# The first batch's preparation written out in engine order, its two head groups staggered, its conversions and table transfers moved

## The chip, the cores and the metric

The kernel runs on one core of one Trainium2 chip. The metric is the device time of one execution in microseconds. The engines of the core are TensorE (PE in the profile, PEld for its weight loads), VectorE (DVE), ScalarE (ACT), GpSimd (POOL) and SyncE (SP, which only issues transfers here).

## The reference

Batch 8, 8 heads, 576 tokens, 64 columns a head, 32 packed queries, model width 512, hidden width 2048, all float32.

```python
p_packed = sm_attn(p, k, v)               # 32 packed queries attend to 576 keys
out = sm_attn(q, p_packed, p_packed)      # 576 queries attend to the 32 packed values
x = out.transpose(0, 2, 1, 3).reshape(B, S, H * D)
X = np.fft.fft(np.fft.fft(x, axis=1), axis=2)
u = x + np.real(X).astype(np.float32)
un = (u - mean(u)) / np.sqrt(var(u) + 1e-06)
return u + np.maximum(un @ w_ch1, 0.0) @ w_ch2
```

## The kernel before

**Accuracy by splitting.** Large products use float32 operands split into a rounded high part (ScalarE, `split`, L97) and the remainder (VectorE or GpSimd, L98): `three` (L230) makes three products of the parts. Names in h and l are such pairs (uh and ul, fh and fl, gh and gl, wr_h and wr_l).

**Front and feed-forward.** `front(b)` (L235) prepares batch b. It works on two groups of four heads, g = 0 and 1, in steps named by letters in ORDER (L40), the first string for batch 0, the second for all others: transfers K, I, V, Q, B, L, W; S scores and exponents; X turned scores; p packed values (with the block diagonals bd, bdh, bdl on GpSimd and ScalarE); d their transposition and split; U the queries' products, turned back into blocks of 32 by VectorE; g the values' spectrum (basis product, multiplication with the tables turn, split into gh and gl); e subtracts the maximum and takes exponents; m subtracts the mean; a scales and transposes; f folds the rows about the middle (even and odd sums); r the folds' last few columns; h splits the folds into fh and fl, and xl, ol. Then follow the wave products (py), their spectrum (pz) and the values (px), the sums pe and qe (L554 to L558), the rows of u with their sum (L561), and statistics (L205: negative mean, squares on ScalarE, a power on GpSimd). EN, EF, ES choose VectorE (0) or GpSimd (1) for some steps: in batch 0 group 1's subtractions, scaling and folds are on GpSimd, and both groups' r.

The generator gives a `yield` where the caller may go on with other work. The main part is `ffn` (L650) for tiles of 512 rows: for each of 16 blocks j of the hidden width an up product (L669), ReLU and split (hh, hl, L673 and L674), and a down product (L684). Every `step` in it advances the next batch's front by one `yield`. Up products write one PSUM bank (tag ph), so one must have been read by hh and hl before the next begins.

**Weights** come as packed words: `fetch` transfers a block to a staging place, `halves_of` makes two ScalarE operations of it (L167, L168), `joined` one VectorE operation (L172). `wsplits` (L640) then splits each block into wr_h on ScalarE and wr_l on GpSimd, for each tile anew. Six blocks are converted before `ffn` begins, the others within the first tile.

**Order of work.** Within `tc.manual_schedule` TensorE, VectorE, ScalarE and GpSimd follow the written order. Outside it, as batch 0's front, the first rows' centring, transposition and split (L744 to L749) and the first conversions are, the framework's scheduler orders each engine's queue by itself, and may draw later written work ahead. `after(n, what)` does a thing n steps later inside `ffn`, and at once before that.

[...]

Of the kernel before, what the change touches and what calls it, by code (L numbers as in the profile page):

```python
# [9 lines left out]
F32 = mybir.dt.float32  # L10
# [7 lines left out]
P = 128  # L18
S = 576
# [12 lines left out]
EF = (((0, 0, 0, 0), (1, 1, 0, 0)), ((0, 0, 0, 0), (0, 0, 0, 0)), ((0, 0, 0, 0), (0, 0, 0, 0)))  # L32
# [7 lines left out]
ORDER = ("K0 K1 I0 V0 V1 Q0 Q1 B0 L0 W0 W1 W2 W3 S X p0 p1 d0 d1 U W4 W5 W6 W7 W8 g0 g1 e0 e1 m0 m1 a0 a1 f0 r0 h0 f1 r1 h1",  # L40
         "S y X y p0 p1 y d0 d1 y g0 y U y g1 y e0 y e1 y y m0 y a0 y m1 y a1 y f0 y r0 y h0 y f1 y r1 y h1 y y")
# [34 lines left out]
def tile_kernel(ctx, tc, kpT, qT, v, w1, w2, tabs, tabR, tabB, tabT, sel, ident_d, out):  # L76
# [45 lines left out]
    def load_base():  # L122
        nc.gpsimd.dma_start(basis, tabB)
        nc.sync.dma_start(turn, tabT)
# [80 lines left out]
    def statistics(key):  # L205
        st, u = stat_of[key], u_of[key]
        nc.vector.tensor_scalar(st[:, 1:2], st[:, 0:1], -1.0 / DM, None, ALU.mult)  # L207

        def squares():
            junk = work.tile([P, DM], F32, tag="tmp", name="junk", bufs=3)  # L210
            nc.scalar.activation(junk, u, AF.Square, bias=st[:, 1:2], scale=1.0, accum_out=st[:, 2:3])  # L211
# [23 lines left out]
    def front(b):  # L235
# [3 lines left out]
        eos, fs, sums = {}, {}, {}  # L239
# [71 lines left out]
        def packed(g):  # L311

            if g not in vts:
                load_values(g)
            vt = vts[g]
            po = bank("po")
            for c in range(5):
                kk = P if c < 4 else D
                for h in range(4):
                    nc.tensor.matmul(  # L320
                        po[h * NPK:(h + 1) * NPK, :D], e1T[g][:kk, c, h * NPK:(h + 1) * NPK],
                        vt[:kk, c, h * D:(h + 1) * D], start=(c == 0), stop=(c == 4),
                        tile_position=(0, h * NPK))
            pp2 = work.tile([P, 2, D], F32, tag="pp2", name="pp2")
            nc.vector.tensor_scalar(pp2, po[:, :D].unsqueeze(1).to_broadcast([P, 2, D]), rinv[g], None, ALU.mult)
            pp2s[g] = pp2
            bd = work.tile([P, 4, D], F32, tag="tmp", name="bd", bufs=3)
            nc.gpsimd.tensor_tensor(bd, pp2[:, 0:1, :].to_broadcast([P, 4, D]),
                                    bmask.unsqueeze(2).to_broadcast([P, 4, D]), ALU.mult)

            def diagonals():
                bdh[g] = work.tile([P, 4 * D], F32R, tag="bdh", name="bdh")
                bdl[g] = work.tile([P, 4 * D], F32R, tag="bdl", name="bdl")
                split(bdh[g], bdl[g], bd.rearrange("p a d -> p (a d)"), nc.gpsimd)

            after(1, diagonals)

        def packed_parts(g):
# [5 lines left out]
            nc.vector.tensor_copy(t, tp[:, :P])  # L344
            ppT[g] = t
# [9 lines left out]
        def queries(*gs):  # L355
# [10 lines left out]
            for c, w in ((1, slice(16, 18)), (0, slice(0, 16))):  # L366
                for g in reversed(gs):
                    nc.vector.transpose(s2s[g][:, w, :].rearrange("p a k -> p (a k)"), s2T[g][c])
# [25 lines left out]
        def values_spectrum(g):  # L394

            hi = work.tile([P, 2, N2], F32R, tag="gh", name="gh")
            lo = work.tile([P, 2, N2], F32R, tag="gl", name="gl")

            TW = (nc.gpsimd, nc.vector)
            prod = []  # L400
            for t in range(2):
                pg = bank("pg")
                nc.tensor.matmul(pg[:, :N2], pph[g], basis[:, t, :], start=True, stop=False)

                nc.tensor.matmul(pg[:, :N2], ppl[g], basis[:, t, :], start=False, stop=True)
# [8 lines left out]
            gh[g], gl[g] = hi, lo  # L414
            after(1, lambda: split(hi, lo, prod[0], TW[TL[min(b, 2)]]))

        def weights(g):

            engs[g].tensor_tensor(s2s[g], s2s[g], broadcast(zs[g]), ALU.mult)
            a = work.tile([P, S], F32, tag="att", name="a", bufs=ATT)  # L420
            nc.vector.transpose(a, s2s[g].rearrange("p a k -> p (a k)"))
            as_[g] = a

        def folded(g):
# [3 lines left out]
            f = work.tile([P, FW], F32, tag="att", name="f", bufs=ATT)  # L428
# [8 lines left out]
            eos[g], fs[g] = eo, f  # L437

        def folded_rest(g):
# [17 lines left out]
            sm.tensor_copy(fe3[:, :, 15:16], ec[:, 143:144].unsqueeze(1).to_broadcast([P, 3, 1]))  # L457
            sm.tensor_copy(fo3[:, :, 30:31], oc[:, 143:144].unsqueeze(1).to_broadcast([P, 3, 1]))
            sm.memset(f[:, FR + 99:FR + 101], 1.0 / 32)
            sm.memset(fo3[:, :, 31:33], 0.0)  # L460
            sm.tensor_scalar(f[:, FA:FA + 33], a[:, 256:289], 2.0, 1.0 / 16, ALU.mult, ALU.add)
            sm.tensor_scalar(f[:, FA + 33:FA + 64], a[:, NE + 256:S], 2.0, 1.0 / 16, ALU.mult, ALU.add)
# [5 lines left out]
        def folded_parts(g):  # L468
# [4 lines left out]
            nc.scalar.copy(fh[g], f)  # L473
            xl[g] = work.tile([P, 256], F32R, tag="xl", name="xl")
# [3 lines left out]
            fl[g] = work.tile([P, FW], F32R, tag="fl", name="fl")  # L478
            nc.vector.tensor_tensor(fl[g], f, fh[g].bitcast(F32), ALU.subtract)

        parts = {"S": lambda _: scores(0, 1), "U": lambda _: queries(0, 1), "X": lambda _: turned_scores(0, 1),
                 "s": scores, "t": turned_scores, "p": packed, "d": packed_parts, "q": queries, "e": less_one, "m": less_mean, "g": values_spectrum, "a": weights, "f": folded, "r": folded_rest,
                 "h": folded_parts,
                 "L": lambda _: load_tables(), "B": lambda _: load_base(), "K": load_keys, "V": load_values,
                 "Q": load_queries, "I": lambda _: nc.sync.dma_start(ident, ident_d),
                 "W": lambda i: fetch(i // 2, i % 2), "D": load_weights}
# [6 lines left out]

        yh, yl, yr = [], [], []
        for t, base in enumerate((0, FO)):
            nr = NRC[t]
            hi = work.tile([P, 2, N2], F32R, tag="att", name="yh", bufs=ATT)
            lo = work.tile([P, 2, N2], F32R, tag="att", name="yl", bufs=ATT)
            for c in range(2):
                py = bank("py")  # L500
                for g in range(2):
                    w = slice(base + c * P, base + (c + 1) * P)
                    three(py[:, :N2], fh[g][:, w], fl[g][:, w], gh[g][:, t, :], gl[g][:, t, :], g == 0, g == 1)
                split(hi[:, c, :], lo[:, c, :], py[:, :N2])
            py = bank("pyr")
            for g in range(2):
                w = slice(base + 256, base + 256 + nr)
                three(py[:nr, :N2], fh[g][:, w], fl[g][:, w], gh[g][:, t, :], gl[g][:, t, :], g == 0, g == 1)
            h = work.tile([P, DM], F32R, tag="tmp", name="yr_h", bufs=3)
            nc.scalar.copy(h[:nr, :N2], py[:nr, :N2])  # L510
            st = work.tile([P, N2], F32R, tag=f"yr{t}", name="yr", bufs=1)
            nc.vector.scalar_tensor_tensor(st[:nr], h[:nr, :N2].bitcast(F32), selB[:nr], py[:nr, :N2],
                                           ALU.mult, ALU.add)
            yh.append(hi)
            yl.append(lo)
            yr.append(st)
            yield

# [30 lines left out]
        for c in range(2):  # L549
            A, Bs = spectrum(0, c), spectrum(1, c)  # L550
            yield
            px = value(xh, xl, slice(1 - c, 256, 2))
            pe = work.tile([P, DM], F32, tag="tmp", name="pe", bufs=3)
            nc.vector.tensor_tensor(halves(pe), halves(px), window(A, allp), ALU.add)  # L554
            px = value(oh, ol, slice(1 - c, 256, 2))
# [3 lines left out]
            for key, sign in (((b, "E", c), 1.0), ((b, "O", c), -1.0)):  # L559
                new_u(key)  # L560
                nc.vector.scalar_tensor_tensor(u_of[key], qe, sign, pe, ALU.mult, ALU.add,  # L561
                                               accum_out=stat_of[key][:, 0:1])
            statistics((b, "E", c))
            statistics((b, "O", c))
            yield (None, "rest")[c]
# [175 lines left out]
    for at in gen0:  # L741
        if at == "rest":
            break
    cur = Turned(tiles[0][1])  # L744
    for i in range(4):
        cur.less(i)
        for move in cur.moves(i):
            move()
        cur.parts(i)  # L749
    spare.clear()  # L750
    rest = gen0
    for j in range(ORDER[0].count("D"), LEAD):
        load_weights(j)
    ready, splits = [], wsplits()
    next(splits)
    next(splits)
# [139 lines left out]
```

## Time and profile before

| | us |
|---|---|
| median of 3 runs | 997.16 |
| their range | 995.86 to 998.61 |
| the profiled execution | 998.08 |
| its span, first to last instruction | 996.3 |

The mean granted clock of TensorE in the profiled execution was 0.983. In rows of a timeline stand the start, the duration, engine, line, operation, out<-in with shapes, a count, and in brackets the idle time before and what ended it. In rows of a table of stretches stand the stretch, its length, then busy time and count of PE, PEld, DVE, ACT and POOL, the granted clock, the share of the DMA engines and GB/s. Of the page's 40 slices each stands for 24.9 us; a digit is a tenth.

### The profile page before, as it was taken

How to read it: one execution, taken by the hardware profiler on the slowest of the kernel's cores; microseconds unless marked ns; L12 is line 12 of the kernel's file. 1: busy time of each engine (PE TensorE's matmuls, PEld its weight loads, DVE VectorE, ACT ScalarE, POOL GpSimd, SP SyncE). 2: the span in 40 equal slices, each digit the busy share in tenths (PEclk: the TensorE clock that was granted, in tenths of full speed). 3: DMA queues.
4: the chain of work that ended last, by engine and by line, in shares of the span. 5: the costliest groups of instructions: out<-in, count | busy, mean ns of one | idle time of the engine just before them, and what ended most of it. 6: DMA issues, size and time to landing. Idle time of an engine off the chain costs nothing.

```text
span 996.3 us, 15070 instructions
## 1 busy us (share of the span) xinstructions
PE 953.2 (96%) x5588; PEld 784.4 (79%) x5588; DVE 552.2 (55%) x1227; ACT 469.9 (47%) x942; POOL 477.1 (48%) x420
## 2 busy tenths in 40 slices
PE   5189999999999999999999999999999999999998
PEld 2077778778887888788887888788878888888886
DVE  4866885559354845577546846594648562123112
ACT  4447786444453445445544445435434453343332
POOL 3705643455346534554445434653555354544443
PEclk9589999999999999999999999999999999999999
DMA  9206552410042002200240024101410010011001
GB/s 357 116 6 231 157 175 65 160 36 1 8 135 74 1 1 89 101 1 16 65 157 1 3 59 134 43 1 50 139 49 1 22 64 1 1 31 54 1 1 43
DMA packets 28170, 65.94 MB, mean 66 GB/s; under 512 B 5494, under 2 KB 12992, under 8 KB 28096
## 3 DMA queue, kind: packets, MB, share of 16 engines
q1 hardware_dynamic: 27120, 63.53, 19.2%
q0 software_dynamic: 976, 1.44, 0.5%
q8 instruction: 44, 0.72, 0.3%
q14 instruction: 30, 0.25, 0.1%
HBM read 48.70 MB, written 9.44 MB: 58 GB/s over the span
## 4 chain that ended last, share of the span: by engine, by line
PE 91%; DVE 4%; ACT 2%; POOL 1%; DMA 1%; issue 1%; DVEq 0%; POOLq 0%; ACTq 0%
PE ph L669 38%; PE acc L684 38%; PE po L320 1%; PE s L263 1%; PE px L233 1%; PE px L232 1%; PE px L231 1%; PE py L231 1%; PE e1tp L297 1%; PE py L232 1%; PE py L233 1%; PE pz L231 1%; PE pz L233 1%; PE pz L232 1%; PE s2T L263 1%
## 5 line engine op out<-in xcount | busy, mean ns | idle before, releaser
L98 POOL TENSOR_TENSOR wr_l<-w1f,wr_h 128x512 fp32r<-128x512 f32 x144 | 199.5, 1386 | 280.7 <-ACT wr_h L97 228.6
L674 DVE SCALAR_TENSOR_TENSOR hl<-ph,hh 128x512 fp32r<-128x512 f32 x144 | 99.1, 688 | 341.3 <-ACT hh L673 340.9
L98 POOL TENSOR_TENSOR wr_l<-w2f,wr_h 128x512 fp32r<-128x512 f32 x144 | 190.3, 1322 | 160.1 <-ACT wr_h L97 153.2
L669 PE MATMUL ph<-uh,wr_h 128*128 128x512 f32 (+1 forms) x580 | 228.6, 395 | 4.3 <-DVE hl L674 2.7
L684 PE MATMUL acc<-wr_h,hh 128*128 128x512 f32 x576 | 226.1, 393 | 0.0
L684 PE MATMUL acc<-wr_l,hh 128*128 128x512 f32 x576 | 225.4, 391 | 0.0
L669 PE MATMUL ph<-uh,wr_l 128*128 128x512 f32 (+1 forms) x580 | 225.4, 389 | 0.0
L684 PE MATMUL acc<-wr_h,hl 128*128 128x512 f32 x576 | 225.2, 391 | 0.0
L669 PE MATMUL ph<-ul,wr_h 128*128 128x512 f32 (+1 forms) x580 | 220.8, 389 | 1.1 <-DVE stat L207 1.1
L673 ACT ACTIVATE hh<-ph 128x512 fp32r<-128x512 f32 x144 | 86.3, 599 | 209.2 <-PE ph L669 195.1
L669 PEld LDWEIGHTS ph<-uh,wr_h 128*128 128x128 f32 x580 | 108.9, 188 | 39.0 <-ACT gh L97 6.1
L669 PEld LDWEIGHTS ph<-uh,wr_l 128*128 128x128 f32 x580 | 108.8, 188 | 23.4 <-POOL wr_l L98 0.3
L684 PEld LDWEIGHTS acc<-wr_h,hl 128*128 128x128 f32 x576 | 108.1, 188 | 23.1
L669 PEld LDWEIGHTS ph<-ul,wr_h 128*128 128x128 f32 x580 | 109.0, 189 | 22.0 <-DVE stat L207 1.3
L684 PEld LDWEIGHTS acc<-wr_h,hh 128*128 128x128 f32 x576 | 108.1, 188 | 22.0
L684 PEld LDWEIGHTS acc<-wr_l,hh 128*128 128x128 f32 x576 | 108.2, 188 | 21.4
L97 ACT CAST wr_h<-w1f 128x512 fp32r<-128x512 f32 x144 | 89.0, 618 | 55.6 <-POOL wr_l L98 52.8
L97 ACT CAST wr_h<-w2f 128x512 fp32r<-128x512 f32 x144 | 88.4, 614 | 10.0 <-PE acc L684 7.2
L231 PE MATMUL py<-gh,fh 128*128 128x258 f32 x64 | 19.5, 305 | 26.3 <-ACT fh L473 26.3
L211 ACT ACTIVATE junk<-ubuf,stat 128x512 f32<-128x512 f32 x36 | 25.6, 714 | 27.6 <-DVE stat L207 27.6
L98 POOL TENSOR_TENSOR gl<-turned,gh 128x516 fp32r<-128x516 f32 x16 | 24.8, 1551 | 27.3 <-ACT gh L97 27.3
L215 POOL TENSOR_TENSOR stat<-stat,mhalf 128x1 f32<-128x1 f32 x36 | 23.6, 671 | 25.6 <-DVE stat L214 25.6
(198 smaller groups left out, 1257.8 us busy)
## 6 DMA issues: line engine op xcount, KB each, us to landing
kp<-kpT SPq DMA_DIRECT2D x16, 608.0 KB, 3.9
out<-ubuf SPq DMA_DIRECT2D x36, 256.0 KB, 2.1
vt<-v SPq DMA_DIRECT2D x14, 640.0 KB, 5.1
wst<-w SPq DMA_DIRECT2D x17, 512.0 KB, 3.6
qt<-qT SPq DMA_DIRECT2D x14, 576.0 KB, 4.9
raw<-flip SPq DMA_DIRECT2D x208, 32.0 KB, 1.8
ubuf<-w SPq DMA_DIRECT2D x9, 512.0 KB, 3.9
w1f<-w SPq DMA_DIRECT2D x3, 512.0 KB, 13.8
```

Source lines behind the costliest of these rows:

```text
L97: nc.scalar.copy(hi, src)
L98: (lo_eng or nc.vector).tensor_tensor(lo, src, hi.bitcast(F32), ALU.subtract)
L211: nc.scalar.activation(junk, u, AF.Square, bias=st[:, 1:2], scale=1.0, accum_out=st[:, 2:3])
L215: nc.gpsimd.tensor_tensor(st[:, 2:3], st[:, 2:3], mhalf, ALU.pow)
L231: nc.tensor.matmul(o, lh, rh, start=first, stop=False)
L232: nc.tensor.matmul(o, lh, rl, start=False, stop=False)
L233: nc.tensor.matmul(o, ll, rh, start=False, stop=last)
L263: nc.tensor.matmul(res[g][c][at, :w.stop - w.start], lhs(g, h), rhs(g, h, w), start=True, stop=True, tile_position=(r, h * NPK))
L669: nc.tensor.matmul(ph[:, t], l[:, c * P:(c + 1) * P], r[:, c, t], start=(n == 0), stop=(n == 11))
L673: nc.scalar.activation(hh[:, :T], ph[:, :T], AF.Relu)
L674: nc.vector.scalar_tensor_tensor(hl[:, :T], ph[:, :T], 0.0, hh[:, :T].bitcast(F32), ALU.max, ALU.subtract)
L684: nc.tensor.matmul(acc[i], l[:, w], r, start=(j == 0 and k == 0), stop=(j == NJ - 1 and k == 2))
```

## The change

Batch 0's front, the first six conversions but for their transfers, the first two weight splits and the first tile's centring and transposition move into `manual_schedule`, in a written order. That order lets the two groups follow each other step by step (first group's e and m before the second group's e and m are through, waves of group 0 before group 1's fold). Steps are cut finer for that: c (block diagonals), l (split of the packed values), u (second group's blocks), G, T, z (the parts of g), w and b (of a), x (xl and ol), P (wave products of one group, six PSUM banks open at once).

Of single operations: basis comes through SP into a staging place and is copied by ScalarE (N); the tables' six GpSimd transfers (L) stand behind the block diagonals; the halves of weight blocks (H) stand between front steps and the joins at their places in the main part; group 1's folds go to VectorE; r's two copies and two doublings go to ScalarE, its two constants to GpSimd ahead of the folds; f lies in the space of uh; centring is ScalarE's; squares and the power of the first rows wait for the first steps of `ffn`. For other batches fl comes before xl and ol, and both rows are made before their statistics; the rest is as it was.

```diff
-EF = (((0, 0, 0, 0), (1, 1, 0, 0)), ...
+EF = (((0, 0, 0, 0), (0, 0, 0, 0)), ...
-ORDER = ("K0 K1 I0 V0 V1 Q0 Q1 B0 L0 W0 W1 W2 W3 S X p0 p1 d0 d1 U W4 W5 W6 W7 W8 g0 g1 e0 e1 m0 m1 a0 a1 f0 r0 h0 f1 r1 h1",
+ORDER = ("K0 K1 I0 V0 V1 Q0 Q1 B0 W0 W1 W2 W3 S t0 t1 p0 p1 d0 d1 l0 l1 U N c0 W4 W5 c1 L0 W6 W7 W8 H0 H1 e0 u G0 e1 "
+         "H2 T0 z0 G1 m0 w0 b0 H3 H4 f0 r0 m1 w1 T1 h0 z1 P0 H5 b1 f1 r1 x0 h1 x1 P1",
...
-        nc.gpsimd.dma_start(basis, tabB)
+        nc.sync.dma_start(spot(0, 2, [P, 2, N2]), tabB)
...
-        after(1, squares)
-        after(2, deviation)
+        now_at = steps[0] if steps[0] is not None else key[2]
+        due.append((now_at + 1, squares))
+        due.append((now_at + 2, deviation))
...
+            if b == 0 and g == 1:
+                nc.scalar.copy(t, tp[:, :P])
+            else:
+                nc.vector.tensor_copy(t, tp[:, :P])
...
-            f = work.tile([P, FW], F32, tag="att", name="f", bufs=ATT)
+            if b > 0:
+                f = work.tile([P, FW], F32, tag="att", name="f", bufs=ATT)
+            else:
+                if g == 0:
+                    fs[None] = work.tile([P, 4, 512], F32, tag="uh", name="f", bufs=1).rearrange("p c t -> p (c t)")
+                f = fs[None][:, g * 1024:g * 1024 + FW]
+                constants(f, nc.gpsimd)
...
+                for o, x in doubled:
+                    nc.scalar.activation(o, x, AF.Copy, scale=2.0, bias=1.0 / 16)
+                for o, x in middles:
+                    nc.scalar.copy(o, x.unsqueeze(1).to_broadcast([P, 3, 1]))
...
+        WAVES = [(0, 0), (1, 0), (0, None), (1, None), (0, 1), (1, 1)]
...
+        def waves_of(g):
+            for at in WAVES:
+                if g == 0:
+                    pys[at] = bank("py")
+                wave(*at, (g,))
+                if g == 1:
+                    wave_split(*at)
...
+        if b == 0:
+            pq = None
+            for c in range(2):
+                px = [side_value(n, c) for n in range(2)]
+                AB = spectrum(0, c), spectrum(1, c)
+                if c == 1:
+                    yield
+                    for key in ((b, "E", 0), (b, "O", 0)):
+                        rows_of(key, *pq)
+                        statistics(key)
+                        yield
+                else:
+                    yield
+                pq = sums(c, lambda n: px[n], *AB)
+            yield
+            for key in ((b, "E", 1), (b, "O", 1)):
+                rows_of(key, *pq)
+                statistics(key)
+                yield
+            yield "rest"
...
-    for at in gen0:
-        if at == "rest":
-            break
...
+    def centred(i):
+        cur.less(i, True)
+        for move in cur.moves(i):
+            move()
+    with tc.manual_schedule(engines=MANUAL):
+        next(gen0)
+        for k in (0, 2):
+            joined(k // 2, k % 2)
+        next(splits)
+        next(splits)
+        next(gen0)
+        next(gen0)
+        centred(0)
+        next(gen0)
+        centred(1)
+        next(gen0)
+        cur.parts(0)
+        cur.parts(1)
+        next(gen0)
+        centred(2)
+        next(gen0)
+        centred(3)
+        cur.parts(2)
+        cur.parts(3)
+        for k in (1, 3, 4, 5):
+            joined(k // 2, k % 2)
+        assert next(gen0) == "rest"
```

More of the change, by code (lines that the diff above doesn't have):

```diff
@@ L392, in less_mean, with values_products, values_turned @@
             zs[g] = z
[L394 to L402, printed above, removed]
+        TW = (nc.gpsimd, nc.vector)
+        def values_products(g):
+            prods[g] = [bank("pg") for t in range(2)]
+            for t, pg in enumerate(prods[g]):
                 nc.tensor.matmul(pg[:, :N2], pph[g], basis[:, t, :], start=True, stop=False)
                 nc.tensor.matmul(pg[:, :N2], ppl[g], basis[:, t, :], start=False, stop=True)
+        def values_turned(g):
+            prod = []
+            for t, pg in enumerate(prods[g]):
                 x = work.tile([P, 2, N2], F32, tag="tmp", name="turned", bufs=3)
@@ new lines, in front, with wave, wave_split @@
+        yh, yl, yr = {}, {}, {}
+        def wave(t, c, gs):
+            nr = NRC[t] if c is None else P
+            w = slice((0, FO)[t] + (256 if c is None else c * P), (0, FO)[t] + (256 + nr if c is None else (c + 1) * P))
+            for g in gs:
+                three(pys[t, c][:nr, :N2], fh[g][:, w], fl[g][:, w], gh[g][:, t, :], gl[g][:, t, :], g == 0, g == 1)
+        def wave_split(t, c):
+            py = pys[t, c]
+            if c is not None:
+                if t not in yh:
+                    yh[t] = work.tile([P, 2, N2], F32R, tag="att", name="yh", bufs=ATT)
+                    yl[t] = work.tile([P, 2, N2], F32R, tag="att", name="yl", bufs=ATT)
+                split(yh[t][:, c, :], yl[t][:, c, :], py[:, :N2])
+                return
+            nr = NRC[t]
+            h = work.tile([P, DM], F32R, tag="tmp", name="yr_h", bufs=3)
+            nc.scalar.copy(h[:nr, :N2], py[:nr, :N2])
+            yr[t] = work.tile([P, N2], F32R, tag=f"yr{t}", name="yr", bufs=1)
+            nc.vector.scalar_tensor_tensor(yr[t][:nr], h[:nr, :N2].bitcast(F32), selB[:nr], py[:nr, :N2],
+                                           ALU.mult, ALU.add)
@@ L491, in front @@
                 parts[x[0]](int(x[1:] or 0))
[L494 to L517, printed above, removed]
+        if b > 0:
+            for t in range(2):
+                for c in (0, 1, None):
+                    pys[t, c] = bank("py")
+                    wave(t, c, range(2))
+                    wave_split(t, c)
+                yield
         def spectrum(t, par):
@@ L547, in halves, with sums @@
             return x.rearrange("p (a c) -> p a c", a=2)
[L549 to L552, printed above, removed]
+        SIDES = ((xh, xl), (oh, ol))
+        def sums(c, px, A, Bs):
             pe = work.tile([P, DM], F32, tag="tmp", name="pe", bufs=3)
-            nc.vector.tensor_tensor(halves(pe), halves(px), window(A, allp), ALU.add)
-            px = value(oh, ol, slice(1 - c, 256, 2))
+            nc.vector.tensor_tensor(halves(pe), halves(px(0)), window(A, allp), ALU.add)
+            px = px(1)
             qe = work.tile([P, DM], F32, tag="tmp", name="qe", bufs=3)
@@ L558, in front, with rows_of, side_value @@
             nc.vector.tensor_tensor(qe[:, 256:512], px[:, 256:512], Bs[:, 1:257], ALU.add)
[L559 to L565, printed above, removed]
+            return pe, qe
+        def rows_of(key, pe, qe):
+            new_u(key)
+            nc.vector.scalar_tensor_tensor(u_of[key], qe, 1.0 if key[1] == "E" else -1.0, pe, ALU.mult, ALU.add,
+                                           accum_out=stat_of[key][:, 0:1])
+        def side_value(n, c):
+            return value(*SIDES[n], slice(1 - c, 256, 2))
+        if b == 0:
+            pq = None
[8 more added lines that the diff above has]
+                        yield
+                else:
+                    yield
[4 more added lines that the diff above has]
+                statistics(key)
+                yield
+            yield "rest"
+        else:
+            for c in range(2):
+                A, Bs = spectrum(0, c), spectrum(1, c)
+                yield
+                pe, qe = sums(c, lambda n: side_value(n, c), A, Bs)
+                for key in ((b, "E", c), (b, "O", c)):
+                    rows_of(key, pe, qe)
+                for key in ((b, "E", c), (b, "O", c)):
+                    statistics(key)
+                yield (None, "rest")[c]
         kr = (b // 2, "R")
```

86 lines of the change are left out of this document (55 added, 31 removed).

## The prediction

> **What bounds the kernel now.** I read the page first (busy times, the 40 slices), then the table of stretches, then the timeline of the first 80 us engine by engine, then the waits. On the page, TensorE is busy nearly all the time, except in the first three slices, where its granted clock falls to half as well:
>
> ```profile
> PE 953.2 (96%) x5588; PEld 784.4 (79%) x5588; DVE 552.2 (55%) x1227; ACT 469.9 (47%) x942; POOL 477.1 (48%) x420
> PE   5189999999999999999999999999999999999998
> PEclk9589999999999999999999999999999999999999
> ```
>
> In the table of stretches TensorE is full from 70 us on:
>
> ```profile
> 70.00:80.00 10.00, 10.00 (x85) 7.97 (x85) 4.72 (x11) 8.45 (x20) 1.84 (x2) 1.00 0.52 180
> ...
> 200.00:300.00 100.00, 100.00 (x551) 82.95 (x550) 62.21 (x143) 47.34 (x97) 46.72 (x38) 1.00 0.13 43
> ```
>
> So only the first batch's preparation can give time, and the change touches little else. The timeline shows the idle stretch and its end, and the point I use as the **mark**: 70.18, where the first up product of the feed-forward part is over and the last rows' spectrum begins.
>
> ```profile
> 46.89 0.58 PE L231 MATMUL py<-gh,fh 128*128 128x258 f32 x1 [25.74 <-ACT fh L473]
> ...
> 70.18 0.28 PE L231 MATMUL pz<-yh,tbh 128*128 128x258 f32 x1
> ```
>
> TensorE stands still for 25.74 us because ScalarE's rounded fold (fh) is late. From the mark on the span is TensorE's, so a microsecond at the mark is a microsecond at the end, unless the feed-forward part then waits.
>
> **Durations for the sum.** These rows of the same timeline carry it. Neighbouring rows of an engine overlap by some 0.06 us, so a 0.69 us operation costs 0.62 in a row of its kind.
>
> ```profile
> 2.51 0.55 POOL L129 DMA_DIRECT2D tbh<-tabs  x1
> 15.29 0.61 POOL L328 TENSOR_TENSOR bd<-pp,bmask 128x256 f32<-128x256 f32 x1 [9.49 <-DVE pp L325]
> 15.93 0.41 ACT L97 CAST bdh<-bd 128x256 fp32r<-128x256 f32 x1 [1.98 <-POOL bd L328]
> 16.41 0.72 POOL L98 TENSOR_TENSOR bdl<-bd,bdh 128x256 fp32r<-128x256 f32 x1 [0.52 <-ACT bdh L97]
> 18.49 1.08 PE L263 MATMUL s2T<-w2f,ppT 64*32 64x512 f32 x4
> 19.67 1.31 DVE L368 STREAM_TRANSPOSE s<-s2T 128x512 f32<-128x512 f32 x2
> 20.74 0.67 ACT L167 ACTIVATE w1f<-w1f 128x512 f32<-128x512 f32 x1 [2.43 <-DMA w1f<-w]
> 20.91 1.86 DVE L409 TENSOR_TENSOR turned<-pg,turn 128x516 f32<-128x516 f32 x3
> 22.69 0.74 DVE L413 TENSOR_TENSOR turned<-turned 128x258 f32<-128x258 f32 x2
> 23.35 0.74 DVE L374 TENSOR_REDUCE m<-s 128x18 f32<-128x576 f32 x1
> 23.86 0.61 ACT L97 CAST gh<-turned 128x516 fp32r<-128x516 f32 x1
> 24.55 1.28 POOL L98 TENSOR_TENSOR gl<-turned,gh 128x516 fp32r<-128x516 f32 x1 [5.60 <-ACT gh L97]
> 24.62 1.82 DVE L375 TENSOR_TENSOR s<-s,m 128x576 f32<-128x576 f32 x1
> 26.47 0.68 ACT L378 ACTIVATE s<-s 128x576 f32<-128x576 f32 x1 [0.18 <-DVE s L375]
> 31.55 0.16 DVE L388 TENSOR_SCALAR d<-z 128x18 f32<-128x18 f32 x1
> 32.31 0.74 DVE L391 TENSOR_TENSOR s<-s,d 128x576 f32<-128x576 f32 x1
> 36.04 1.53 POOL L391 TENSOR_TENSOR s<-s,d 128x576 f32<-128x576 f32 x1
> 40.42 0.78 DVE L421 STREAM_TRANSPOSE a<-s 128x576 f32<-128x576 f32 x1 [1.05 <-POOL s L419]
> 41.12 0.42 DVE L431 TENSOR_TENSOR eo<-a 128x287 f32<-128x287 f32 x1
> 42.03 0.28 DVE L434 TENSOR_TENSOR f<-eo 128x128 f32<-128x128 f32 x1
> 45.63 1.27 POOL L449 TENSOR_TENSOR f<-eo 128x45 f32<-128x45 f32 x4
> 49.04 0.84 ACT L473 CAST fh<-f 128x776 fp32r<-128x776 f32 x1 [2.20 <-POOL f L462]
> 49.91 0.97 DVE L479 TENSOR_TENSOR fl<-f,fh 128x776 fp32r<-128x776 f32 x1 [1.29 <-ACT fh L473]
> 57.34 0.69 DVE L554 TENSOR_TENSOR pe<-px,spec 128x512 f32<-128x512 f32 x1 [1.02 <-PE px L233]
> 58.84 0.69 DVE L561 SCALAR_TENSOR_TENSOR ubuf<-qe,pe 128x512 f32<-128x512 f32 x1
> 60.25 0.72 ACT L211 ACTIVATE junk<-ubuf,stat 128x512 f32<-128x512 f32 x1 [0.87 <-DVE stat L207]
> 65.43 0.47 DVE L602 TENSOR_SCALAR un<-ubuf,stat 128x512 f32<-128x512 f32 x1
> ```
>
> One behaviour decides much of the sum. The subtraction at 24.62 took 1.82 us on VectorE while GpSimd worked from 24.55 to 25.83; the like one at 32.31 took 0.74. I read this as: a VectorE operation with both inputs in SBUF waits until a running GpSimd operation ends (25.83 plus 0.6 is its end), and the other way round (the two weight low parts of a later fence, 3.54 for two). [...]
>
> **The change, in the written order.** Queues are now followed strictly; I walk through them with the rows above.
>
> *Transfers.* The turning tables' 258 KB (basis) go onto SP behind the queries, with a ScalarE copy (as gh, 0.61) hidden behind the query product; the six other table transfers leave the first microseconds and come 15 us later on GpSimd, sels behind the fifth and sixth weight block. SP's queue gains 0.65 us of transfer ahead of turn and the weights, but the other tables (1.15 MB: four of 224 KB, two of 126) leave in front of them, so weights and queries land earlier. The table of stretches, the DMA part and the timeline give rate, sizes and who waits:
>
> ```profile
> 4.00:5.00 1.00, 0.33 (x9) 0.33 (x10) 0.00 (x0) 0.00 (x0) 1.00 (x3) 1.00 1.00 404
> ```
>
> ```profile
> tbh<-tabs POOLq DMA_DIRECT2D x2, 224.0 KB, 9.1
> ```
>
> ```profile
> 6.26 0.18 PEld L263 LDWEIGHTS s1t<-kp 64*32 64x32 f32 x6 [1.20 <-DMA kp<-kpT]
> ```
>
> For 1.20 us TensorE waited for the second keys; at 404 GB/s the 258 KB, which were the first on GpSimd's queue, are 0.6 us of that. The queries' products end at 19.57 (row 18.49 plus 1.08); less 0.6 for the keys, and 0.6 more for the two groups' products alternating (bounds 0 and 1.0): 18.4.
>
> *First group.* VectorE: tails 0.4, first block 0.65, maximum 0.68, subtraction 0.68: 20.8. ScalarE is behind: copy of the basis to 17.3, the block diagonals with GpSimd in turn (0.41, 0.72, 0.61, 0.41) to 19.4, then two weight blocks, four times 0.65, to 22.0, and only now the two exponent operations: 23.4. GpSimd: last low part to 20.2, six issues of 0.55 to 23.5, then the second group's subtraction (1.47) to 25.0. VectorE meanwhile: second block and maximum to 22.1, two products 1.25 to 23.4; the two sums (0.67) take the lock after GpSimd, 25.0 to 25.7. Then sum 0.68, three small ones 0.45, subtraction and scaling 1.36, transposition 0.72: upright at 28.9. ScalarE: exponents of the second group to 26.4, a weight block to 27.7, gh to 28.3; GpSimd's gl to 29.7 holds the first folds back by 0.8. Folds: 0.36 twice, 0.22 four times, to 31.3; GpSimd's six rest operations (0.32 each) from 30.4 to 32.3; what GpSimd did besides (copies, doublings) is ScalarE's now and lies beside them.
>
> *Second group.* GpSimd's subtraction to 33.8, its scaling to 35.6 after half of VectorE's sums, the other half to 36.0, fl 0.9 to 36.9, transposition to 37.6, against 41.20 before. gl to 38.2, two folds to 38.9 (on VectorE now), GpSimd's rest to 40.8, fh from 40.9. Before, it began at 49.04: **8.1 us gained**, since a whole group's fold and rest stood behind the first one's on GpSimd.
>
> *Fold to first sum.* Before 8.3 us (49.04 to 57.34). Now fh 0.84, fl 0.9, six waves of three products (18 instead of 18 and 18, the first group's being done), value products and spectrum, copy: 7.8. First sum at 48.7, **8.6 gained**.
>
> *First sum to last transposition.* Before, un of the last tile ends at 65.90, 8.6 us after the first sum. Now VectorE loses the four un (ScalarE has them) but the two weight low parts on GpSimd, which were long done, come now; their row before:
>
> ```profile
> 32.39 3.54 POOL L98 TENSOR_TENSOR wr_l<-w1f,wr_h 128x512 fp32r<-128x512 f32 x2 [1.31 <-ACT wr_h L97]
> ```
>
> VectorE: twice 1.4 for sums, four times 0.83 for rows with their statistics, twice 0.62 for ul: 7.4. The first two row operations have both inputs in SBUF and meet the two low parts: 2.2 in waits (bounds 0 and 2.7). ScalarE's last un 0.7: 59.0, **6.9 gained**. Transpositions 0.5 to 0.6, first half product 1.7 (it no longer runs ahead, but covers the last split), second 1.45: 62.8. **7.4 gained at the mark.**
>
> *Feed-forward part.* The four squares (0.72 and a read of 0.19 each) and their pow are moved behind the mark: 3.6 us more on ScalarE, in the stretch 70 to 80, where it was busy 8.45 of 10. What waits for that: the second up product's rounding hh, whose low part frees the only bank in which the third up product can start.
>
> ```profile
> 78.61 0.69 DVE L674 SCALAR_TENSOR_TENSOR hl<-ph,hh 128x512 fp32r<-128x512 f32 x1 [2.83 <-ACT hh L673]
> ...
> 80.42 0.48 PE L669 MATMUL ph<-uh,wr_h 128*128 128x512 f32 x1
> ```
>
> Slack there is 1.1 us; of ScalarE's 1.55 idle some 1.1 lies ahead of it. 3.6 less 2.2 is a stall of **1.4 us lost** (bounds 0 and 3.6). The other batches keep the order of work but for a few small moves (low parts after fl, statistics after both rows): nothing.
>
> Sum: 7.4 less 1.4, **6.0 us**. The profiled execution took 998.08 (span 996.3 and 1.8 around it), 0.92 over the median of 997.16 and inside the three runs: 992.1 on its scale, **991.2** on the median's. A difference below 0.3%, 3 us, could not be told from no change.
>
> **The rivals.**
>
> *A, the lock hardly bites* (chance 0.20): small GpSimd operations and the gaps between VectorE's let both pass. For it: VectorE's folds at 41.12 to 42.3 kept their pace beside GpSimd's small operations. Against: row 24.62. Then the sums of the first group no longer push GpSimd's low part and folds (0.7), the second group is upright right after its scaling (1.6), gl does not hold its folds (0.6), the rows pass the weights' low parts (2.2): 5.1 more, 986.1.
>
> *B, the start of the feed-forward part takes it back* (0.12): this is the one that ends slower. Not only the squares (3.6), but the third weight block's rounding (0.6) and four joins on VectorE (2.5, at 0.62 like a row operation of that shape, and 1.3 behind GpSimd's low part) now stand in the queues just ahead of or behind the first up product, where the scheduler had done them in the idle stretch. If none of it finds cover, 8.0 is paid: 997.16 less 7.4 plus 8.0 gives 997.8, and more if the third product's lateness is handed to the fourth. It decides from 7.4 us of stall. Against: from the mark to the third up product TensorE has other products for 10.2 us (70.18 to 80.42).
>
> *C, GpSimd is the bound* (0.12): the table issues cost twice 0.55 in a busy stretch (3.3 more on GpSimd, of which about half, 1.7, reaches the folds), its low parts 0.4 more each, the rest 0.5: 3.0 less gained, 994.2. [...] That the tables then come late is no danger: they are needed at about 47.
>
> **How the numbers follow.** Forecast 0.56, A 0.20, B 0.12, C 0.12. The forecast's own range is 988 to 994.5, from the bounds of stall, row waits and query products. With A at one end and most of B at the other the range is 985.8 to 997.5. Faster by over 0.3% (below 994.2): most of the forecast (0.51), A, half of C: 0.77. Slower by over 0.3%: the worse half of B, 0.07. Within: 0.16.
>
> **What would show it.** Right: fh of the second group near 41, first sum near 49, the mark near 63; the first row operation on VectorE stretched beyond 1 us by GpSimd; a wait of 1 to 2 us of the third up product for hl or wr_l. Wrong: fh near 36 (A), the mark near 63 but PE gaps of over 5 us in the next 30 (B), table issues well over 0.55 and the second group's subtraction after 26 (C), or any fold standing behind a weight transfer on ScalarE, which I left out.

## The result and the profile after

| | us |
|---|---|
| before, same chip | 996.51, median of 4 (995.02 to 998.61) |
| after | 989.83, median of 4 (989.33 to 990.03) |
| ratio after to before | 0.9931, 95% interval 0.9911 to 0.995 |
| profiled execution after | 990.03 (span 988.3) |

Faster by 6.7 us by the medians, where 6.0 was predicted (991.2), and by 8.0 between the two profiled spans (996.3 and 988.3). The page of the changed kernel, to be laid beside that of before:

```profile
PE 952.2 (96%) x5588; PEld 783.8 (79%) x5588; DVE 555.2 (56%) x1224; ACT 474.4 (48%) x956; POOL 469.1 (47%) x409
PE   4589999999999999999999999999999999999998
```

TensorE's work is what it was; its second slice went from 1 tenth to 5. The timeline of the changed kernel, first 75 us (start, duration, engine, line, operation):

```profile
17.16 0.59 PE L266 MATMUL s2T<-w2f,ppT 64*32 64x512 f32 x1
...
20.66 0.78 POOL L131 DMA_DIRECT2D tbh<-tabs  x1
...
24.15 1.18 POOL L397 TENSOR_TENSOR s<-s,m 128x576 f32<-128x576 f32 x1
...
28.13 0.46 DVE L476 TENSOR_TENSOR eo<-a 128x287 f32<-128x287 f32 x1
...
28.59 1.50 POOL L100 TENSOR_TENSOR gl<-turned,gh 128x516 fp32r<-128x516 f32 x1 [3.27 <-ACT gh L99]
28.87 1.37 DVE L478 TENSOR_TENSOR f<-eo 128x128 f32<-128x128 f32 x1
...
35.91 0.77 DVE L460 STREAM_TRANSPOSE a<-s 128x576 f32<-128x576 f32 x1
...
37.76 0.37 DVE L478 TENSOR_TENSOR f<-eo 128x128 f32<-128x128 f32 x1
...
39.42 0.84 ACT L529 CAST fh<-f 128x776 fp32r<-128x776 f32 x1 [0.74 <-POOL f L498]
...
47.57 0.69 DVE L631 TENSOR_TENSOR pe<-px,spec 128x512 f32<-128x512 f32 x1 [0.38 <-ACT spec L609]
...
48.62 2.98 POOL L100 TENSOR_TENSOR wr_l<-w1f,wr_h 128x512 fp32r<-128x512 f32 x2 [9.24 <-ACT wr_h L99]
48.96 1.51 DVE L640 SCALAR_TENSOR_TENSOR ubuf<-qe,pe 128x512 f32<-128x512 f32 x1
...
50.58 1.57 DVE L640 SCALAR_TENSOR_TENSOR ubuf<-qe,pe 128x512 f32<-128x512 f32 x1
...
54.49 0.39 PE L780 MATMUL ph<-uh,wr_h 128*128 128x256 f32 x1 [0.67 <-ACT uh L99]
...
56.05 1.52 ACT L711 ACTIVATE un<-ubuf,stat 128x512 f32<-128x512 f32 x2 [1.61 <-DVE stat L209]
...
56.83 1.97 PE L720 MATMUL untp<-ident,un 128*128 128x128 f32 x8 [0.15 <-ACT un L711]
...
60.99 0.28 PE L234 MATMUL pz<-yh,tbh 128*128 128x258 f32 x1
...
61.47 1.64 POOL L100 TENSOR_TENSOR wr_l<-w2f,wr_h 128x512 fp32r<-128x512 f32 x1 [9.87 <-ACT wr_h L99]
61.86 1.80 DVE L174 SCALAR_TENSOR_TENSOR w2f<-w2f 128x512 int32<-128x512 int32 x1
...
62.50 0.71 ACT L213 ACTIVATE junk<-ubuf,stat 128x512 f32<-128x512 f32 x1
...
63.20 0.64 ACT L609 COPY spec<-pz 128x258 f32<-128x258 f32 x2
63.58 0.68 DVE L785 SCALAR_TENSOR_TENSOR hl<-ph,hh 128x512 fp32r<-128x512 f32 x1
63.61 0.18 PEld L266 LDWEIGHTS s<-kp 64*32 64x32 f32 x14 [0.59 <-ACT spec L609]
...
64.63 0.50 PE L780 MATMUL ph<-uh,wr_h 128*128 128x512 f32 x1
...
72.18 0.41 PE L303 MATMUL e1tq<-ident,e 128*64 128x128 f32 x2 [0.21 <-DVE xa L686]
...
72.35 0.48 PE L780 MATMUL ph<-uh,wr_h 128*128 128x512 f32 x1
```

The second group's fh starts at 39.42 (before 49.04), the first sum at 47.57 (57.34), the mark is 60.99 (70.18), and the third up product begins at 72.35 (80.42): 9.6, 9.8, 9.2 and 8.1 us earlier.

**Not all of the 8.1 can be put down to the change's steps.** The timeline of before, from the value products to the queries' products:

```profile
14.64 1.45 PE L320 MATMUL po<-w2f,e1T 128*32 128x64 f32 x40
...
17.18 1.06 PE L263 MATMUL s2T<-w1f,ppT 64*32 64x512 f32 x1
```

And the same part, in the same order, in the experiment before_folds (below), which edits nothing ahead of 40 us:

```profile
14.51 0.90 PE L320 MATMUL po<-w2f,e1T 128*32 128x64 f32 x40
...
17.16 0.61 PE L263 MATMUL s2T<-w2f,ppT 64*32 64x512 f32 x4
```

The same forty value products took 1.45 us in one execution and 0.90 in the other, a query product 1.06 and 0.59, and the queries' products end at 19.57 and at 17.77. I read this as TensorE's clock, full from about 14.5 us on in the one and only from about 20.3 in the other (its values' products shorten from 0.42 to 0.28 us there), although the clock column prints 1.00 in that stretch for both. The profiled execution of before was thus 1.8 us late, the changed kernel's was not (17.16 plus 0.59 is 17.75), and 8.1 less 1.8 leaves 6.3: between the prediction's 6.0 and the medians' 6.7. Whether the change has a part in this clock is open. Of the fourteen profiles in this case three have it late, with query products of 1.05 us and more (before and, below, tables_first and tables_and_split); all three are among the six kernels that issue the table transfers first, but the other three of the six don't have it. Later distances are therefore given from the end of the queries' products too.

### The profile page after: what moved, and what is told of

It is laid out like the page before. It is cut to its first block, busy times and chain, and to the rows that moved or that the text cites. A ratio compares the mean times of both kernels' runs of the same rounds, so it can differ in the third digit from the quotient of the medians.

```text
span 988.3 us, 15063 instructions
## 1 busy us (share of the span) xinstructions
PE 952.2 (96%) x5588; PEld 783.8 (79%) x5588; DVE 555.2 (56%) x1224; ACT 474.4 (48%) x956; POOL 469.1 (47%) x409
## 4 chain that ended last, share of the span: by engine, by line
PE 90%; DVE 4%; ACT 3%; DMA 1%; issue 1%; POOL 0%; SPq 0%; DVEq 0%; ACTq 0%; POOLq 0%
PE ph L780 38%; PE acc L795 38%; PE po L323 1%; PE py L236 1%; PE py L234 1%; PE py L235 1%; PE px L234 1%; PE px L236 1%; PE px L235 1%; PE e1tp L300 1%; PE s L266 1%; PE s2T L266 1%; PE pz L234 1%; PE pz L236 1%; PE pz L235 1%
## 5 line engine op out<-in xcount | busy, mean ns | idle before, releaser
L100 POOL TENSOR_TENSOR wr_l<-w1f,wr_h 128x512 fp32r<-128x512 f32 x144 | 194.6, 1352 | 280.1 <-ACT wr_h L99 237.9
L100 POOL TENSOR_TENSOR wr_l<-w2f,wr_h 128x512 fp32r<-128x512 f32 x144 | 192.3, 1336 | 173.1 <-ACT wr_h L99 166.3
L234 PE MATMUL py<-gh,fh 128*128 128x258 f32 (+2 forms) x96 | 29.1, 303 | 14.4 <-ACT fh L529 14.4
L236 PE MATMUL py<-gh,fl 128*128 128x258 f32 (+2 forms) x96 | 29.0, 302 | 2.6 <-DVE fl L531 2.6
```

The source lines that it names most:

```text
L100: (lo_eng or nc.vector).tensor_tensor(lo, src, hi.bitcast(F32), ALU.subtract)
L234: nc.tensor.matmul(o, lh, rh, start=first, stop=False)
L236: nc.tensor.matmul(o, ll, rh, start=False, stop=last)
```

## The experiments

Twelve runs in three groups of four; the kernel before, run beside each group, took 996.11, 995.17 and 995.05 us (medians). The first four ask whose the gain is. One theory: the written order is the larger part, the single edits the smaller. Its rival: the scheduler finds such an order by itself, and the single edits bring the time.

**front_free.** The changed kernel, with the first batch's front given back to the scheduler.

```diff
-    with tc.manual_schedule(engines=MANUAL):
+    if True:
         next(gen0)
```

> The changed kernel with its front's written order taken away: all finer steps, the folds on VectorE and the moved transfers stay, but the framework's scheduler orders the first batch's queues again. Theory 1 (the order of the queues is the larger part: weight conversions and the weight low parts get ahead of steps on the path, as before): the second group's rounded fold begins at 42 to 46 instead of 39.4, the mark (end of the first up product) at 64 to 67 instead of 61.0, time 993 to 996. Theory 2 (the single edits do it, whatever the order): mark within 1 us of 61, time 989 to 991.

Measured 990.13 (989.86 to 993.4, 5 runs), ratio 0.9946 (0.9929 to 0.9964). Its timeline:

```profile
40.91 0.84 ACT L529 CAST fh<-f 128x776 fp32r<-128x776 f32 x1 [0.69 <-DVE f L481]
...
61.31 0.28 PE L234 MATMUL pz<-yh,tbh 128*128 128x258 f32 x1
```

The fold is 1.5 us later than in the written order, the mark 0.3. The mark alone flatters this kernel: from the second fh to the first sum it takes 5.99 us here (40.91 to 46.90) and 8.15 in the changed kernel, because TensorE's clock rose at about 41.5 here and at about 45 there (the products shorten from 0.42 to 0.28 us; see the last section). The times differ by 0.3 us by the medians and by 1.5 by the ratios, and the intervals overlap widely; by the interval of its own ratio this kernel keeps 3.6 to 7.1 us of gain without the written order. So the theory of the written order as the larger part fell: the two estimates give it 0.3 to 1.5 us of the 6.7, and neither can be told from nothing.

**before_folds.** The kernel before, with one edit of the change: group 1's folds on VectorE.

```diff
-EF = (((0, 0, 0, 0), (1, 1, 0, 0)), ...
+EF = (((0, 0, 0, 0), (0, 0, 0, 0)), ...
```

> The kernel before with one edit: the second group's two long folds on VectorE instead of GpSimd. Theory 1: they leave 1.3 us on GpSimd's path (its rest operations can begin at 44.4 instead of 45.6), so the rounded fold starts near 47.8 instead of 49.0 and the time falls by about 1.2 us, not told from none. Theory 2 (the folds are the main part of the gain): 3 us or more.

Measured 993.05 (992.03 to 995.54, 10 runs), ratio 0.9971 (0.9959 to 0.9982): 3.1 us, more than twice the expected. Its timeline:

```profile
47.13 0.84 ACT L473 CAST fh<-f 128x776 fp32r<-128x776 f32 x1 [0.72 <-POOL f L458]
...
48.02 0.53 PE L231 MATMUL py<-gh,fh 128*128 128x258 f32 x1 [0.15 <-ACT fh L473]
48.39 0.28 PE L232 MATMUL py<-gl,fh 128*128 128x258 f32 x1
...
53.03 0.69 DVE L554 TENSOR_TENSOR pe<-px,spec 128x512 f32<-128x512 f32 x1 [0.80 <-PE px L233]
```

From the end of the queries' products to the second fh it is 29.36 us here and 29.47 before: up to the fold the edit gained 0.1. From fh to the first sum it is 5.90 against 8.30: 2.4 gained there. The wave products last 0.28 each here from 48.39 on; before, those behind its second fh last 0.42. The second group's waves follow the first's after a wait of 0.15 us (0.52 before), and the clock rises at 48 us, while in the profile of before it rises only after 54. folds_and_squares, below, has the same 5.90 (47.22 to 53.11). That the smaller gap brings the clock up sooner fits these profiles; it isn't shown apart from chance.

**squares_now.** The changed kernel, with the first rows' squares and power made at once.

```diff
         now_at = steps[0] if steps[0] is not None else key[2]
+        if steps[0] is None:
+            squares()
+            deviation()
+            return
         due.append((now_at + 1, squares))
```

> The changed kernel, but the first four rows' squares and powers are taken at once, in the front, as before. Theory 1 (the deferral pays, since they stand between rows and centring there): mark 2 to 3.6 us later, the stretch from the mark to the third up product 0.3 to 1.1 shorter than 11.36, time 991 to 993. Theory 2 (they cost ScalarE the same behind the mark): time as the changed kernel within 0.6 us.

Measured 992.36 (991.64 to 993.4, 5 runs), ratio 0.9961 (0.9947 to 0.9976). The mark moves from 60.99 to 64.98, and the third up product from 72.35 to 75.81. Its table of stretches (length, PE, PEld, DVE, ACT, POOL, clock, DMA, GB/s):

```profile
60.00:62.00 2.00, 0.67 (x5) 0.42 (x4) 0.51 (x2) 1.72 (x5) 0.55 (x1) 1.00 0.00 0
...
64.00:66.00 2.00, 2.00 (x11) 2.00 (x11) 2.00 (x3) 1.04 (x2) 1.48 (x1) 0.50 0.00 0
```

ScalarE is busy 1.72 of 2 us where TensorE waits, and behind the wait the clock is lower as well (1.00 from 60 to 62 us, 0.50 from 64 to 66), so the second half of the up product runs at half. Putting the squares off is worth about 2.5 us in this kernel. The run also shows what the squares cost behind the mark:

```profile
67.49 1.06 PE L270 MATMUL s<-kp 64*32 64x512 f32 x16
```

With the squares made ahead, the next batch's scores (s) take 1.06 us, as before the change, where the changed kernel needs 1.79; and from the second to the third up product it is 7.33 (68.48 to 75.81), as before (7.32), where the changed kernel needs 7.72.

**folds_gpsimd.** The changed kernel, with group 1's folds back on GpSimd (the EF line above, reversed).

> The changed kernel with the second group's two long folds on GpSimd again. Theory 1 (GpSimd's queue is on the path of the second group): rounded fold begins 1.0 to 1.5 us after 39.4, time 991 or so. Theory 2 (VectorE and GpSimd block one another, so it is the sum of their work that counts): no later than 39.9, time 990.

Measured 990.8 (989.86 to 990.97, 4 runs), ratio 0.9943 (0.9927 to 0.996). fh begins at 40.28, 0.9 later, the first sum at 47.96, 0.4 later, the mark at 61.23, 0.2 later. In both kernels the clock stays at half till about 45 us (products of 0.42 us up to there, 0.28 behind it), and more than half of the difference is gone by the first sum. About 1 us by the medians, within the intervals.

**folds_and_squares.** If single edits bring the gain, then these two in the kernel before should bring much of it: the folds on VectorE, and the squares put off.

```diff
-        after(1, squares)
-        after(2, deviation)
+        now_at = steps[0] if steps[0] is not None else key[2]
+        due.append((now_at + 1, squares))
+        due.append((now_at + 2, deviation))
```

> The kernel before with two edits: the second group's folds on VectorE, and the squares and powers of the first rows left to the first steps of the feed-forward part. Theory 2 (the single edits make the gain; undoing the deferral cost 2.5 us, the folds alone gave 3.1): 990 to 991.5. Theory 1 (the finer steps, the stagger and the transfers carry the rest): 992.5 or more, the deferral giving little without them.

Measured 995.16 (993.86 to 996.07, 11 runs), ratio 0.9998 (0.9989 to 1.0007): nothing gained, 2.1 us worse than the folds alone by the medians, 2.7 by the ratios. Its timeline:

```profile
62.11 0.56 PE L670 MATMUL ph<-uh,wr_h 128*128 128x256 f32 x1
62.47 0.42 PE L670 MATMUL ph<-uh,wr_l 128*128 128x256 f32 x1
```

In before_folds the first half of the up product ran at 58.46, ahead of the last tile's un; here the scheduler puts the whole product behind that un (60.66), at 62.11, and it starts at the low clock (0.42 for a product of 0.28). The mark is 66.55, against 64.63 in before_folds. So this theory fell too: the edit that is worth 2.5 us in the changed kernel costs 2 in the old one, and the edits' worths don't add.

**tables_first.** Now the two places where the change seemed to cost something. First the tables: their transfers back into the first microseconds.

```diff
-... B0 W0 W1 W2 W3 S t0 t1 p0 p1 d0 d1 l0 l1 U N c0 W4 W5 c1 L0 W6 ...
+... B0 L0 W0 W1 W2 W3 S t0 t1 p0 p1 d0 d1 l0 l1 U N c0 W4 W5 c1 W6 ...
```

> The changed kernel with the six table transfers issued first again, right after the turning tables. Theory 1 (they held the path behind queries and weights): the second keys land no earlier than in the changed kernel (6.38), weights land up to 2.9 us later, the first conversion waits, the time rises by 0.5 to 1.5. Theory 2 (their 3.5 us of issuing on GpSimd between 20.66 and 24.15 is what counts): the second group's subtraction begins near 21.6 instead of 24.15, and the time falls by up to 1.

Measured 987.7 (986.96 to 988.88, 5 runs), ratio 0.9924 (0.9911 to 0.9938). Its timeline:

```profile
18.44 1.06 PE L266 MATMUL s2T<-w2f,ppT 64*32 64x512 f32 x1
...
20.78 0.67 ACT L169 ACTIVATE w1f<-w1f 128x512 f32<-128x512 f32 x1 [0.54 <-DMA w1f<-w]
...
23.43 1.16 POOL L397 TENSOR_TENSOR s<-s,m 128x576 f32<-128x576 f32 x1 [2.36 <-DVE m L396]
...
29.82 0.37 DVE L478 TENSOR_TENSOR f<-eo 128x128 f32<-128x128 f32 x1
```

This profiled execution drew the late clock: its queries' products end at 19.50, 1.75 later than in the changed kernel. Still the second fh is no later (39.30), because GpSimd, free of six issues, takes the second group's subtraction 0.7 earlier although it waited 2.36 for VectorE, and gl no longer stretches the first fold (0.37 instead of 1.37). The price of the early transfers is 0.54 us of waiting for a weight block. The ratios of the two kernels overlap.

**late_split.** Then the second weight split, whose low part stretches a row operation, behind the first product's parts, and three joins into the first step of ffn.

```diff
         next(splits)
-        next(splits)
...
-        for k in (1, 3, 4, 5):
-            joined(k // 2, k % 2)
+        joined(0, 1)
+        next(splits)
...
+                if t == 0 and i == 0:
+                    for n in (3, 4, 5):
+                        joined(n // 2, n % 2)
```

> The changed kernel with the second weight block's split and three of the four last joins moved behind the last transposed rows and the first hl. If VectorE's waits for GpSimd's lock and for the joins are on the path: the second of the first two row operations takes 0.7 instead of 1.57 us, the second up product starts 0.7 earlier after the mark, and the time falls by 1.2 to 1.6 us. If other work is late next: within 0.4.

Measured 988.59 (988.13 to 989.14, 5 runs), ratio 0.9933 (0.992 to 0.9945). Its timeline:

```profile
49.41 0.68 DVE L640 SCALAR_TENSOR_TENSOR ubuf<-qe,pe 128x512 f32<-128x512 f32 x1
...
62.16 1.09 PE L266 MATMUL s<-kp 64*32 64x512 f32 x14 [0.79 <-ACT spec L609]
...
63.18 0.50 PE L780 MATMUL ph<-uh,wr_h 128*128 128x512 f32 x1
```

The second row operation is back to 0.68 (1.57) and the mark at 58.43, but from there to the second up product it is 4.75 instead of 3.64. On ScalarE the rounding of the third weight block waits 1.96 us for its join, so that all behind it comes later after the mark: hh, two squares, and the spectrum's copy, for which TensorE waits 0.79. Three of the four joins are out of the way of hl here, and the loss is larger, not smaller. From the first sum to the mark the edit gains 1.4 (12.04 against 13.42), and 1.1 of it is lost there; the rest of the early mark is the clock's (last section). No gain is shown in the time.

**warm_pe.** The clock looked like the next thing to have: 80 products whose result is not read, behind the values' products (G1).

```diff
+        def keep_warm():
+            idle = psf.tile([P, 512], F32, tag="ph", name="idle")
+            for _ in range(80):
+                nc.tensor.matmul(idle[:, :N2], basis[:, 0, :P], basis[:, 0, :], start=True, stop=True)
```

> The changed kernel with 80 products more, whose result nothing reads, on TensorE between the queries and the first fold, to keep its clock up. If the half clock counts (wave products 0.21 us apart at 36 to 45): products 0.12 apart there, first sum 0.6 to 0.9 us earlier, time lower by as much. If VectorE's low parts pace the waves: first sum at most 0.2 us earlier, time the same.

Measured 988.74 (988.0 to 989.62, 5 runs), ratio 0.9935 (0.9922 to 0.9947). The clock was 0.68 from 30 to 35 us and 0.50 from 35 to 45: lost again before the waves began. The mark is 61.19: no effect.

**after_again.** The changed kernel once more, as the measure for the last group.

> The changed kernel itself, beside the others on one chip. Since the kernel before took 995.2 on the chip of the last four runs and 996.1 to 996.5 on the others: the changed kernel 6 to 7 us under the kernel before of this chip.

Measured 988.93 (988.08 to 990.32, 6 runs), ratio 0.9934 (0.9921 to 0.9948), the result again: 6.1 us by the medians.

**warm_long.** As warm_pe, with 130 products, up to the first group's waves.

> The changed kernel with 130 idle products instead of 80, so that TensorE is busy until about 36, when the first group's wave products really run (80 ended near 29, and the clock was down again by 35). If the clock paces the second group's waves: they follow 0.12 apart in every run, first sum near 46 instead of 47.57, time 1.0 to 1.7 us under the changed kernel of this chip. If VectorE's low parts pace them: within 0.4.

Measured 988.93 (988.29 to 990.4, 6 runs), ratio 0.9936 (0.9923 to 0.995): the same as without. Its rows are in the last section: the first group's waves ran at full clock and were done 2 us before the second group's could begin, and for most of those the clock was down again.

**tables_and_split.** tables_first and late_split together.

> The changed kernel with the table transfers first and the late second split and joins. If the two gains are of different waits (GpSimd's issues before the second group's subtraction; its low parts before the rows): 1.5 to 3 us under the changed kernel of this chip. If they only took the place of one another, or the earlier mark is waited away at the second up product (it lost 1.9 of 2.6 there): 0.5 to 1.

Measured 987.07 (986.95 to 988.86, 6 runs), ratio 0.992 (0.9906 to 0.9934): the fastest of all, 1.9 us below the changed kernel of the same group (988.93). The intervals still overlap, and late_split alone shows no gain, so the 1.9 is rather the tables'. Its profiled execution took 988.86, with a query product at 1.06 again; four others took 986.95 to 987.10 and one 988.82. The step between them, 1.8, is the size of the late clock at the queries' products; those others have no trace.

**all_three.** tables_and_split with 115 idle products.

> Tables first, late split and joins, and 115 idle products. If the three add: 2.5 to 4 us under the changed kernel of this chip, about 985. If ScalarE's work behind the mark is late next: no more than tables_and_split.

Measured 988.56 (987.28 to 989.45, 6 runs), ratio 0.9927 (0.9912 to 0.9941). The mean clock is 0.995 to 0.997, and the time is no shorter than without them (1.5 us longer by the medians, with intervals that overlap): the 985 of the first expectation did not come.

## Why the prediction was right, step by step

The mechanism held: the gain comes out of the idle stretch ahead of the fold, and a part is given back up to the third up product. One term of the sum, the queries' products, was wrong, and the waits by which ScalarE's squares cost time were others than forecast. The steps, each as the distance from the one before:

| step | before | predicted | measured |
|---|---|---|---|
| queries' products end | 19.57 | 18.4 | 17.75 |
| from there to the second fh | 29.47 | 22.5 | 21.67 |
| to the first sum | 8.30 | 7.8 | 8.15 |
| to the end of the last un | 8.56 | 10.3 | 10.00 |
| to the mark | 4.28 | 3.8 | 3.42 |
| to the third up product | 10.24 | 11.6 | 11.36 |

- **Queries' products.** Wrong in both parts. The second keys come no earlier: TensorE loads them at 6.37 (6.26 before), after a wait of 1.38 (1.20). And alternating the groups is worth nothing: the old order reaches 17.77 in before_folds. The 1.8 us are the clock's, as read above.

```profile
6.37 0.20 PEld L266 LDWEIGHTS s1t<-kp 64*32 64x32 f32 x11 [1.38 <-DMA kp<-kpT]
```

- **To the second fh.** The large term: 7.8 gained, 7.0 forecast from the same point. Of the 7.8, 2.7 lie ahead of the second group's transposition (40.42 before, 35.91 now) and 5.1 behind it: from there to fh it was 8.62 and is 3.51. Before, the first group's folds (41.12) came only after that transposition, and GpSimd did the first group's rest and then the second's folds and rest from 41.28 to 49.01; now the first group's folds begin at 28.13, 7.8 us ahead of it. So the reason that the prediction gave, one group's fold and rest standing in the other's way, is what the rows show. The issues took 0.55 to 0.78 each from 20.66 on, and the subtraction came at 24.15, close to the 23.5 reckoned, so the doubled issues of rival C did not come, nor its 3 us. Before, with VectorE busy for only 0.23 us beside them (at 5.18), the six took 0.54 to 0.58 each from 2.51 on; now VectorE was at work beside all six, and no run shows an issue at the twice 0.55 that C reckoned with.
- **The lock**, the wait for one another that the prediction read from its row 24.62, bit where it was forecast: the fold at 28.87 took 1.37 beside gl, the second group's, at 37.76, 0.37; the row operations at 48.96 and 50.58 took 1.51 and 1.57 beside the two weight low parts, against 0.68 without one (late_split). Rival A, which lets both pass, is out. That the ends coincide (28.59 plus 1.50 is 30.09, and 28.87 plus 1.37 is 30.24) agrees with that reading, in which the one operation waits until the other ends. The two products of pg, one of whose inputs lies in PSUM, did not wait: 1.23 together from 32.45 on, beside GpSimd's subtraction from 32.10 to 33.26, and 1.28 from 21.46 on, beside table issues alone.
- **To the mark.** Right in sum, wrong in one step: the first half of the up product still runs ahead, at 54.49, before the last transposition at 56.83, though it is written behind it. Within a written block the order was kept; here the scheduler let work of one block pass that of another.
- **The stall.** 1.1 us against 1.4 forecast, from the cause that was forecast, the squares on ScalarE, but through other waits. From the mark to the second up product it takes 3.64 (2.92 before), from there to the third 7.72 (7.32 before: 73.10 to 80.42).

```profile
73.10 0.49 PE L669 MATMUL ph<-uh,wr_h 128*128 128x512 f32 x1
```

The first 0.7: on ScalarE two squares (the second at 62.50) stand ahead of the spectrum's copies, which begin at 63.20, 2.2 us after the mark (1.05 before). The weight loads of the next batch's scores wait 0.59 for such a copy (63.61), the scores take 1.79 instead of 1.06, and the second up product starts behind them. The other 0.4: hh of the second up product begins 5.48 us after that product (4.88 before), so hl and, behind it on VectorE, xa are later too, and the transposition at 72.18 waits 0.21 for xa. The third up product itself doesn't wait for hl, as the prediction had it: hl ends at 71.42, with 0.9 us to spare. In squares_now, without these squares, the scores' delay and the 0.4 are gone.

Of rival B's mechanisms the joins do exist: hl at 63.58 stands on VectorE behind four of them, the last of which took 1.80 because GpSimd's low part held the lock from 61.47 to 63.11. But hl ends at 64.26, and without the scores' delay of 0.73 the second up product would have started at 63.90; so the joins alone could have held it up by some 0.4 at most, hidden behind the squares' 0.7, and nothing near the 8.0 that would turn the result.

- **The sum.** From the queries' products on: 7.8 and 0.15 gained, 1.4 lost, 0.9 gained, 1.1 lost, 6.3 in all. That this lies so near the forecast is partly luck: 1.2 of the 6.0 were forecast for the queries' products, where nothing but the clock was gained, and the steps behind them were forecast at 4.8 and came to 6.3.

What stays open is which of the finer edits carries the large term. It is not mainly the written order as such (0.3 to 1.5 us by the estimates) and not the folds alone (about 1 us in the changed kernel, 0.1 up to the fold in the old one). The stagger of the groups goes with the gain: in front_free, too, the first group's folds (32.70) begin ahead of the second group's transposition (36.34), and from there to fh it is 4.57; in before_folds they begin after it (40.14 and 39.43), and it is 7.70. But the stagger, the column copies on ScalarE and the splitting of steps were not tried singly.

## What to carry to other kernels

Ask of an edit what its neighbours' order is when it is made: two edits that gained 3 and 2.5 us in their own surroundings gained nothing together in the old order. Before two profiles are subtracted, compare a stretch that the change doesn't touch, row by row; here 1.8 of 8.0 us was, as I read the rows, a clock that came up late in one of them. And when transfers are issued by an engine that also computes (here 0.55 to 0.78 us of GpSimd for each), issue them while that engine waits anyway: the change moved six issues from an idle to a busy stretch, and undoing that is part of the fastest kernel.

## What the runs showed of the hardware

**The clock of one and the same kernel differs from execution to execution, and 1.7 to 1.8 us hang on each place.** The first place is that of the queries' products, above. The second is the waves of the second group. The changed kernel's table of stretches:

```profile
38.00:40.00 2.00, 1.85 (x9) 1.55 (x7) 1.66 (x6) 1.26 (x4) 1.38 (x5) 0.50 0.00 0
...
42.00:44.00 2.00, 2.00 (x11) 2.00 (x11) 1.23 (x3) 1.19 (x4) 0.00 (x0) 0.50 0.01 4
```

late_split's, which does the same work up to there:

```profile
38.00:40.00 2.00, 2.00 (x12) 1.90 (x10) 2.00 (x7) 1.08 (x5) 1.84 (x6) 0.58 0.00 0
...
42.00:44.00 2.00, 2.00 (x18) 2.00 (x19) 1.78 (x6) 1.76 (x5) 0.00 (x0) 1.00 0.01 4
```

11 products in 2 us against 18, and 8.15 us from the second fh to the first sum against 6.47 (39.92 to 46.39). In late_split the clock rose at 39.5, some 3 us after the first group's waves began; in the changed kernel 3.8 us of such waves, from 36.05 to 39.9, did not raise it, and it came at about 45. The six runs of after_again sort by it: mean clock 0.989 to 0.990 for 988.08 to 988.60, 0.986 for 989.25 to 990.32. So the point of rise varies between executions; what sets it no run here shows.

**Idle products did not hold the clock over a wait of 2 us.** The table of stretches of warm_long:

```profile
38.00:40.00 2.00, 0.21 (x2) 0.00 (x0) 1.62 (x6) 1.26 (x4) 1.34 (x5) 1.00 0.00 0
40.00:42.00 2.00, 1.24 (x7) 1.04 (x8) 1.64 (x3) 0.52 (x2) 0.00 (x0) 0.92 0.00 0
42.00:44.00 2.00, 2.00 (x11) 2.00 (x11) 1.43 (x4) 1.19 (x4) 0.00 (x0) 0.50 0.01 4
```

TensorE stood still from 38.2 to 40.3, and the clock fell at about 41.7, when the products were running again. The mean clock of the run rose to 0.994 to 0.998 with the time unchanged: the full clock lay on the idle products and on waves that had to wait for the second group in any case. A mean clock alone doesn't say that the work ran faster.
